# Query tiles 3 and 4 and y tiles 2 and 3 turned by DRAM and VectorE instead of TensorE, with VectorE's turns in PSUM banks

## The chip, the cores and the metric

One core of a Trainium2 chip runs the whole program. The metric is the device time of one execution in microseconds (us); the time of the kernel before is the median of 3 runs.

## What is computed

Two layers, each a linear-attention block followed by a gated MLP that mixes the rows. S = 2048 rows, D = 512 features, 32 heads of 16, Fh = 896, all in fp32.

```python
def A(x, wqkv, wo):                       # linear attention
    q, k, v = split_heads(x @ wqkv)       # 32 heads of 16
    phi = lambda t: where(t > 0, t + 1, exp(t)) + 1e-6
    kv = einsum("hsd,hse->hde", phi(k), v); z = phi(k).sum(rows)
    o = einsum("hqd,hde->hqe", phi(q), kv) / (phi(q) . z + 1e-6)
    return merge_heads(o) @ wo
def B(x, w_in, w_sp, b_sp, w_out):        # gated MLP with spatial mixing
    z = gelu(x @ w_in)
    z1, z2 = z[..., :896], layernorm(z[..., 896:])
    g = w_sp @ z2 + b_sp[:, None]         # over the 2048 rows
    return (z1 * g) @ w_out
for _ in range(2):
    x = x + A(layernorm(x), wqkv, wo)
    x = x + B(layernorm(x), w_in, w_sp, b_sp, w_out)
```

## The kernel before

**Tiling.** The rows are 16 tiles of 128 (NT = 16). An fp32 operand of a matmul is split into a high part (ScalarE, `high`, L220) and a low part (VectorE, `low`, L223), and a product takes three matmuls (`mm3`, L234 to L236: high by high, high by low, low by high). SBUF is handed out in slots: pages (`pg`, 128 x 512), quads (`qd`), bigs (`bg`); PSUM is 8 banks. Each kind has a list of free slots, used in turn. There is no scheduler: every engine runs its instructions in the order in which the code issues them, and a DMA queue (SP's above all) takes its transfers in that order too.

**Stages of a layer.** P1 makes keys, queries and the sums of the attention. P2 (`class P2`) goes over the tiles once more. P4 and its neighbours do the mixing by w_sp in products that are divided further, and the output product.

**P2.** For tile i: the scaled query (`a`, `a2_den`, `a2_mul`, L856 to L877) is turned, so that features lie on the partitions, and split (`b_high`, `b_low`): "q tile i". `c` multiplies it by W2 (12 matmuls), `c2` adds it to x (L911) and takes the statistics (L365, L367 on VectorE, L369 to L372 on POOL), `c3` normalises (ScalarE, L378): "y tile i". That is turned and split as well (`d_high`, `d_low`, into a quad). From it `e` makes the gate half z2 by 24 matmuls of 448 columns, with gelu on ScalarE (L1076) and a normalisation, and `f` makes the other half for four tiles at once. P2's loop runs over steps s; step s issues q tile s, c of tile s-1, y's turn of tile s-2, c3 of tile s-1, `a2` of tile s+2 and e of tile s-3. `run` is layer 0's loop, `run2` layer 1's. From s = 6 on, `run` also issues one or two groups of `f` a step (FONE). POOL and SP in layer 0 also work on sums of parts of w_sp (`sums.tick`: w_sp loads at L202, s stores at L1679) during P2.

**Turning.** `class Turn` knows two ways. A tile named in `by_pe` is turned by four PE transposes (`transposes`, L390) into a PSUM bank, which the split reads; the query's are copied into another order of features first (ScalarE, L421). Any other tile is stored to DRAM on SP (L426), loaded back in another shape on SP (`load`, L202), and turned by one VectorE STREAM_TRANSPOSE (L455) into its `home`: a page for queries, a row-tile slot called z_y for y (`ZHome`), a bank for P1's tiles. Before, q tiles 0 to 4 and y tiles 0, 1, 2, 3 and 15 are in `by_pe`, in both layers. In `run`, where a y tile is in `by_pe` (`late`, L1367), its `d_high` and `d_low` come ahead of `c3`; where it isn't, behind it and behind `a`. `run2` has the same as `ahead`. The load of a turned tile is issued in step s with `qturn.load(s + 2)` and `xturn.load(s - 1)` in layer 0, `qturn.load(s + 1)` at the start of a step in layer 1.

**Mixing's start.** `run` of the mixing class calls for every group of matmuls g: `sp(g + 2)`, which splits a quad of w_sp (ScalarE L1775, VectorE L1778), then `zahead`, which splits pages of z some groups ahead, then `mm(g)` (L2000 to L2002).

Of the kernel before, what the change touches and what calls it, by code (L numbers as in the profile page):

```python
# [19 lines left out]
NT = S // P  # L20
# [98 lines left out]
ACTFROM = 10  # L119
E4LATE = 14  # L120
AHEAD = 14
SPN = 3
LOAD2 = (9, 10, 11, 14)
DVE2 = {12: 1, 13: 1, 14: 2, 15: 2, 16: 2}
# [34 lines left out]
def mixer_kernel(ctx: ExitStack, tc: tile.TileContext, x_in, wqkv, wo_d, win1_d, win2_d, wsp_d, bsp_d, wout_d,  # L159
# [9 lines left out]
    pages = Slots(main, "pg", 22)  # L169
    quads = Slots(main, "qd", 6)  # L170
    bigs = Slots(main, "bg", 4)
    banks = Banks(psum, "bank", 8)
# [231 lines left out]
    class Turn:  # L404

        def __init__(self, name, by_pe, always=False, inbank=False, home=None, copy=True):
            self.name, self.by_pe, self.always, self.inbank, self.home = name, by_pe, always, inbank, home
            self.copy = copy  # L410
            self.held, self.d, self.raw, self.made = {}, {}, {}, {}

# [35 lines left out]
        def pre(self, i):  # L448

            if i in self.made or i not in self.raw:  # L450
                return
            r = self.raw.pop(i)
            home = self.home(i) if self.home else banks if self.inbank else pages
            y = home.get([P, 4, P])
            nc.vector.transpose(y.rearrange("p c (t m) -> p m c t", m=4), r.rearrange("p (m c j) -> p m c j", m=4, c=4))  # L455
            pages.put(r)
            self.made[i] = y, home


    class P1:  # L460
        def __init__(self, L):
            self.L = L
            self.st = 2 * L
            self.x, self.ms, self.xT, self.pk, self.kb, self.r, self.xhl = {}, {}, {}, {}, {}, {}, {}
            self.wk, self.wq = w_square(wqkv, 512), w_square(wqkv, 0, True)
            self.win2 = InSeven() if L else w_in2()
            self.later = deque(range(NT - DEFER, NT))
            self.turn = Turn(f"xt{L}", range(3) if L == 0 else (), False, True)
            self.G = None
            self.zacc = None  # L470
            self.half = None
# [359 lines left out]
    class P2:  # L831
        def __init__(self, p1):
            self.L = L = p1.L
            self.p1 = p1
            self.win1, self.win2 = None if L else w_in1(), p1.win2
            self.ws = deque()
            self.wf = deque([] if not L else [w1parts[f] for f in list(range(NF)) * 2 + [0, 6, 1, 2, 6]]
                            + [w1sums[f, m] for m in range(2) for f in range(3)]
                            + [[t[:, 256:512] for t in w1parts[f + 3]] for f in range(3)])
            self.draw, self.S, self.fdone, self.qhome, self.zacc, self.meant = {}, {}, None, {}, {}, set()  # L840
            self.qturn, self.xturn = Turn(f"qt{L}", range(5), True), Turn(f"yt{L}", (0, 1, 2, 3, NT - 1), home=ZHome, copy=bool(L))
            self.qp, self.qT, self.x, self.ms, self.xB, self.z, self.zms = {}, {}, {}, {}, {}, {}, {}
            self.fq = deque()
            self.fnext = []
            self.A, self.u, self.y = {}, {}, {}
# [484 lines left out]
        def run(self, sums):  # L1330
# [4 lines left out]
            for s in range(1, NT + 3):  # L1335
                if s in (15, 16, 17):
                    self.first_a(s - 15)
                self.loadx(s + 1)
                if s in self.qturn.by_pe:
                    self.c(s - 1)  # L1340
                    self.b_high(s)
                    self.c2(s - 1)
                    self.p1.late_phi_b()
                    self.b_low(s)
                    if s >= 2:
                        self.d_high(s - 2)
                        self.d_low(s - 2)
                    self.p1.late()
                    self.c3(s - 1)
                    self.a2(s + 2)  # L1350
                    self.p1.late_phi_a()
                    self.a(s + 3)
                    sums.tick()
                else:
                    if s < NT:
                        self.b_high(s)
                    self.a2_den(s + 2)
                    if s < NT:
                        self.b_low(s)
                    if s <= NT:  # L1360
                        self.c(s - 1)
                        self.c2(s - 1)
                    if s == NT:
                        quads.put(*self.W2)
                        pages.put(self.zbc)
                    self.a2_mul(s + 2)
                    late = s - 2 in self.xturn.by_pe and s <= NT or AHEAD <= s <= NT  # L1367
                    if s in (NT, NT + 1):
                        self.e(s - 3)
                        self.e2(s - 3)  # L1370
                    if late:
                        self.d_high(s - 2)
                        self.d_low(s - 2)
                    if s <= NT:
                        self.c3(s - 1)
                    self.a(s + 3)
                    if s <= NT + 1 and not late:
                        self.d_high(s - 2)
                        self.d_low(s - 2)
# [99 lines left out]
        def run2(self):  # L1479
            late = self.p1  # L1480
            for s in range(1, NT + 3):
# [2 lines left out]
                self.qturn.load(s + 1)  # L1484
                if s in EXTRA:
                    self.wfetch()
                if s in self.qturn.by_pe:
                    self.c(s - 1)
                    self.b_high(s)
                    self.c2(s - 1)  # L1490
# [217 lines left out]
    class P4:  # L1708
# [622 lines left out]
        def run(self, nxt):  # L2331
            p2 = self.p2
            early = nxt is None
            self.zmade = 0
            n = 0
            for _ in p2.tail():
                n += 1
                if n == 1:
                    self.sums.store()
                self.zahead(n - 1)  # L2340
                self.sp(n - 1)
                if n < 3:
                    self.fetch(n + 3)
            self.zahead(3)
            if not early:
                assert len(self.sums.todo) == LEFT
            self.gb = [bigs.get([P, NF, 512]) for _ in range(NCHK)]
            n = len(self.steps)
            for g in range(n):
                p, k = self.steps[g]  # L2350
                self.fetch(g + 5)
                evac_first = p == "P6" and k == HT - 1
                div_first = p in self.div and k == 13 and p == "P4"
                if not evac_first and not div_first:
                    self.sp(g + 2)
                    self.zahead(g + (3 if p == "P5" else 4))
                self.mm(g)
                if evac_first:
                    self.evac(p)
                    self.sp(g + 2)  # L2360
                if not early and g == TFIRST - 1:
                    self.sums.fetch()
                if not early and TFIRST <= g <= TFIRST + LEFT:
                    self.sums.tick()
                if nxt is not None:
                    self.sums.halve(PARTS.get((p, k), -1), self.mark)
                if p in self.div:
                    if p == "P4" and k == 0 and "P5" in self.div:
                        for j in range(2):
                            nc.gpsimd.tensor_tensor(self.unit(2 + j, 6), self.unit(2 + j, 6), self.unit(j, 6), op=OP.add)  # L2370
                    if k % 2 == 1:
                        self.evac_div(p, self.SEVEN[k // 2])
                    if div_first:
                        self.sp(g + 2)
                    if k == 13 and p == "P4":
                        self.gq.extend((n, f) for n in range(2) for f in range(3))
                    if p == "P5":
                        if k > 10 and k < 13:
                            self.carry(12 - k)
                        if k == 0 or k % 2 == 1:  # L2380
                            self.tick()
                        self.wseven(p, {6: 3, 9: 4, 10: 5, 11: 6, 13: 7}.get(k, -1))
                        if k == 13:
                            self.gq.extend([(n, 3) for n in range(2)] + [(n, 4 + f) for n in range(2) for f in range(3)])
                    continue
                if p == "P1" and k == 6:
                    self.ask(3)
                self.tick()
                if p == "P3":
                    if k == FIRST:  # L2390
                        self.first()
                self.wseven(p, k)
                if p == "P7" and k == HT - 1 and self.div:
                    self.sp(g + 3)
                if k == HT - 1 and not evac_first:
                    self.evac(p, (0,) if p == "P3" else (0, 1))
            pages.put(*self.bs)
            self.out7(nxt)
# [80 lines left out]
```

## Time and profile before

| | |
|---|---|
| median of 3 runs | 1343.82 us (1343.27 to 1344.25) |
| the profiled execution | 1341.83 us |
| its span, first to last instruction | 1340.1 us |
| PE busy | 1334.2 us, 6533 instructions |
| VectorE (DVE) busy | 1074.3 us, 1687 |
| ScalarE (ACT) busy | 739.8 us, 1250 |
| GpSimd (POOL) busy | 464.1 us, 611 |
| moved by DMA | 291.34 MB, 217 GB/s on the mean |
| P2 of layer 0 / of layer 1, the steps spoken of | about 151 to 185 us / 833 to 854 us |

A timeline row is: start, duration (us), engine, line, operation, result and operand by the program's names, partitions by elements, and, in brackets, how long the engine was idle before it and what ended that. "x8" joins eight neighbours. A matmul's duration overlaps with the next one's, so starts tell its cost. "PE bank L619 <- DVE ones_f L185: 1.0, 1, 1.0" in the list of waits reads: PE, about to write a bank at L619, waited for VectorE's result, 1.0 us in all, once, longest 1.0.

### The profile page before, as it was taken

What the parts mean: (1) busy time and instruction counts of PE and PEld (TensorE: products, weight loads), DVE (VectorE), ACT (ScalarE), POOL (GpSimd) and SP (SyncE); (2) the same over time, 40 slices, a digit from 0 to 9 for tenths busy, and PEclk for the clock granted to TensorE, in tenths of its full rate; (3) what the DMA queues carried; (4) which work ended last, traced back from release to release, by engine and by line L of the source; (5) the groups of instructions that cost most, each with busy time, mean ns of one, the idle gap of its engine ahead of it and who ended that gap; (6) DMA issues with size and microseconds to landing.
All of it is one profiled execution on the core that took longest, in us unless ns stands there. A gap on an engine that the chain in (4) does not pass through costs nothing.

```text
span 1340.1 us, 19243 instructions
## 1 busy us (share of the span) xinstructions
PE 1334.2 (100%) x6533; PEld 1138.6 (85%) x6533; DVE 1074.3 (80%) x1687; ACT 739.8 (55%) x1250; POOL 464.1 (35%) x611
## 2 busy tenths in 40 slices
PE   9999999999999999999999999999999999999998
PEld 7888888888888888889988888888888888888898
DVE  7779877767899889898866777777689758899885
ACT  5774544347742265345666655557687333666464
POOL 3765675533036400301422443544441012122021
PEclk9999999999999999999999999999999999999999
DMA  5898489977779986884864552678767455579354
GB/s 184 281 313 275 166 286 313 306 223 250 250 270 378 324 263 216 287 302 79 184 159 138 137 131 88 211 237 269 226 203 246 155 171 174 178 242 322 115 78 65
DMA packets 172594, 291.34 MB, mean 217 GB/s; under 512 B 14544, under 2 KB 53456, under 8 KB 172240
## 3 DMA queue, kind: packets, MB, share of 16 engines
q1 hardware_dynamic: 153376, 250.92, 56.2%
q0 software_dynamic: 18976, 39.07, 13.7%
q8 instruction: 51, 0.84, 0.3%
q14 instruction: 47, 0.39, 0.1%
q10 hardware_dynamic: 144, 0.13, 0.0%
HBM read 205.39 MB, written 101.45 MB: 229 GB/s over the span
## 4 chain that ended last, share of the span: by engine, by line
PE 95%; DMA 2%; DVE 2%; ACT 1%; issue 0%; POOL 0%; SPq 0%; DVEq 0%; ACTq 0%
PE bank L234 13%; PE bank L236 13%; PE bank L235 13%; PE bank L2001 12%; PE bank L2000 12%; PE bank L2002 12%; PE bank L2198 3%; PE bank L2199 3%; PE bank L2200 3%; PE bank L990 1%; PE bank L991 1%; PE bank L992 1%; PE bank L1163 1%; PE bank L1162 1%; PE bank L1161 1%; PE bank L390 1%
## 5 line engine op out<-in xcount | busy, mean ns | idle before, releaser
L2001 PE MATMUL bank<-qd,pg 128*128 128x512 f32 x736 | 286.5, 389 | 0.6 <-DVE qd L1778 0.6
L2002 PE MATMUL bank<-qd,pg 128*128 128x512 f32 x736 | 286.3, 389 | 0.0
L2000 PE MATMUL bank<-qd,pg 128*128 128x512 f32 x736 | 286.3, 389 | 0.0
L1775 ACT ACTIVATE qd<-qd 128x1024 fp32r<-128x1024 f32 x142 | 149.2, 1053 | 125.2 <-PE bank L2002 101.7
L1778 DVE TENSOR_TENSOR qd<-qd,qd 128x1024 fp32r<-128x1024 f32 x132 | 168.6, 1279 | 37.6 <-ACT qd L1775 37.4
L236 PE MATMUL bank<-qd,pg 128*128 128x512 f32 x448 | 174.7, 390 | 0.0
L2001 PEld LDWEIGHTS bank<-qd,pg 128*128 128x128 f32 x736 | 138.1, 188 | 29.5 <-DVE qd L1778 1.0
L2002 PEld LDWEIGHTS bank<-qd,pg 128*128 128x128 f32 x736 | 138.1, 188 | 28.8
L2000 PEld LDWEIGHTS bank<-qd,pg 128*128 128x128 f32 x736 | 138.1, 188 | 28.6
L2041 POOL TENSOR_TENSOR bg<-bg,pg 128x512 f32<-128x512 f32 x28 | 49.8, 1780 | 187.6 <-ACT qd L1775 92.5
L234 PE MATMUL bank<-qd,pg 128*128 128x512 f32 x264 | 103.2, 391 | 0.3 <-ACT pg L220 0.2
L235 PE MATMUL bank<-qd,pg 128*128 128x512 f32 x264 | 102.9, 390 | 0.0
L236 PEld LDWEIGHTS bank<-qd,pg 128*128 128x128 f32 x448 | 84.1, 188 | 18.2 <-DVE pg L223 0.4
L1684 POOL TENSOR_TENSOR pg<-pg,pg 128x512 f32<-128x512 f32 x48 | 70.8, 1476 | 68.7 <-DMA pg<-in_wsp_dram 66.6
L369 POOL TENSOR_SCALAR rs<-mv 128x1 f32<-128x1 f32 x76 | 23.8, 313 | 172.7 <-DVE mv L367 169.0
L2200 PE MATMUL bank<-wo,qd 128*128 128x256 f32 x288 | 81.5, 283 | 0.0
L2198 PE MATMUL bank<-wo,qd 128*128 128x256 f32 x276 | 78.1, 283 | 0.0
L2199 PE MATMUL bank<-wo,qd 128*128 128x256 f32 x276 | 78.0, 283 | 0.0
L220 ACT ACTIVATE pg<-pg 128x512 fp32r<-128x512 f32 (+1 forms) x86 | 50.0, 592 | 45.8 <-DVE pg L1869 19.9
L223 DVE TENSOR_TENSOR pg<-pg,pg 128x512 fp32r<-128x512 f32 (+1 forms) x84 | 54.5, 657 | 11.3 <-ACT pg L220 10.6
L549 POOL TENSOR_TENSOR pg<-pg,pg 128x512 f32<-128x512 f32 x30 | 39.9, 1331 | 55.8 <-DVE pg L543 53.9
L234 PE MATMUL bank<-bg,qd 128*128 128x448 f32 x160 | 59.0, 369 | 0.0
(297 smaller groups left out, 3358.2 us busy)
## 6 DMA issues: line engine op xcount, KB each, us to landing
qd<-s SPq DMA_DIRECT2D x62, 512.0 KB, 4.6
qd<-in_wsp_dram SPq DMA_DIRECT2D x40, 512.0 KB, 4.0
qd<-hP SPq DMA_DIRECT2D x40, 512.0 KB, 4.6
pg<-z SPq DMA_DIRECT2D x56, 256.0 KB, 5.1
pg<-in_wsp_dram SPq DMA_DIRECT2D x52, 256.0 KB, 4.4
s<-pg SPq DMA_DIRECT2D x48, 256.0 KB, 4.0
z<-pg SPq DMA_DIRECT2D x40, 256.0 KB, 3.5
pg<-w POOLq DMA_DIRECT2D x38, 256.0 KB, 4.9
```

The costliest lines, as they stand in the source:

```text
L234: nc.tensor.matmul(out, ah, bh, start=start, stop=False)
L235: nc.tensor.matmul(out, ah, bl, start=False, stop=False)
L236: nc.tensor.matmul(out, al, bh, start=False, stop=stop)
L1684: nc.gpsimd.tensor_tensor(t, a, b, op=OP.add)
L1775: self.mark = nc.scalar.activation(w[:, 0], r, AF.Copy)
L1778: nc.vector.tensor_sub(w[:, 1], r, w[:, 0].bitcast(F32))
L2000: m(out, h[:, o], w[:, 0, j, :], start=start, stop=False, skip_group_check=True)
L2001: m(out, h[:, o], w[:, 1, j, :], start=False, stop=False, skip_group_check=True)
L2002: m(out, l[:, o], w[:, 0, j, :], start=False, stop=stop, skip_group_check=True)
L2198: m(out, A, x, start=start and f == 0, stop=False, skip_group_check=True)
L2199: m(out, A, y, start=False, stop=False, skip_group_check=True)
L2200: m(out, B, x, start=False, stop=stop and f == 2, skip_group_check=True)
```

## The change

Query tiles 3 and 4 and y tiles 2 and 3 leave `by_pe` in both layers: they go by DRAM and VectorE like the later tiles. The branch of a step that the query's `by_pe` selected is now selected by s < 5, so steps 1 to 4 keep their order of work. `Turn` gets `banked`, a set of tiles whose VectorE turn is written into a PSUM bank: q tiles up to 12 in both layers (in place of pages), y tiles up to 12 in layer 0 (in place of z_y); P1's tiles have banks as before. As y tile 3 is no longer in `by_pe`, step 5 issues its `d_high` and `d_low` behind `c3`. In layer 0's mixing the first six groups call `zahead` three groups ahead, not four.

```diff
+QBANK = 13, 13
+YBANK = 13
...
-        def __init__(self, name, by_pe, always=False, inbank=False, home=None, copy=True):
+        def __init__(self, name, by_pe, always=False, home=None, copy=True, banked=()):
...
-            home = self.home(i) if self.home else banks if self.inbank else pages
+            home = banks if i in self.banked else self.home(i) if self.home else pages
...
-            self.turn = Turn(f"xt{L}", range(3) if L == 0 else (), False, True)
+            self.turn = Turn(f"xt{L}", range(3) if L == 0 else (), banked=range(NT))
...
-            self.qturn, self.xturn = Turn(f"qt{L}", range(5), True), Turn(f"yt{L}", (0, 1, 2, 3, NT - 1), home=ZHome, copy=bool(L))
+            self.qturn, self.xturn = Turn(f"qt{L}", range(3), True, banked=range(QBANK[L])), Turn(f"yt{L}", (0, 1, NT - 1), home=ZHome, copy=bool(L), banked=() if L else range(YBANK))
...
-                if s in self.qturn.by_pe:
+                if s < 5:
...
-                    self.zahead(g + (3 if p == "P5" else 4))
+                    self.zahead(g + (3 if p == "P5" or not early and g < 6 else 4))
```

(The line with `if s in self.qturn.by_pe` changes in both `run` and `run2`. Lines of the changed kernel behind the two constants have numbers two higher.)

Where it moves instructions, three places. The first is SP's queue in layer 0's P2, step 3: x_2 is the sum stored by c3(2), qt_5 the fifth query tile on its way through DRAM, yt_2 the y tile, s the parts of w_sp's sums. Before:

```order
L917 DMA x_2_81<-pg_191_1693 128x512
L426 DMA qt_5_1904<-pg_206_1842 128x4x128
L1679 DMA s_145<-pg_198_1760 128x512
L1679 DMA s_2_131<-pg_197_1758 128x512
L202 DMA pg_214_1910<-in_wsp_dram 128x512
L202 DMA pg_215_1912<-in_wsp_dram 128x512
L202 DMA pg_216_1914<-in_wsp_dram 128x512
L202 DMA pg_217_1918<-qt_5_1904 128x512
L202 DMA pg_218_1961<-in_win_dram 128x512
L202 DMA pg_219_1963<-in_x_dram 128x512
```

and in the changed kernel:

```order
L919 DMA x_2_81<-pg_191_1693 128x512
L428 DMA yt_2_1900<-pg_212_1898 128x4x128
L428 DMA qt_5_1907<-pg_205_1844 128x4x128
L1681 DMA s_145<-pg_197_1760 128x512
L1681 DMA s_2_131<-pg_196_1758 128x512
L204 DMA pg_214_1913<-in_wsp_dram 128x512
L204 DMA pg_215_1915<-in_wsp_dram 128x512
L204 DMA pg_216_1917<-in_wsp_dram 128x512
L204 DMA pg_217_1921<-qt_5_1907 128x512
L204 DMA pg_218_1923<-yt_2_1900 128x512
L204 DMA pg_219_1966<-in_win_dram 128x512
```

y 2's store has come in ahead of query 5's store, its load behind query 5's load, where the w_in load stood.

The second place is ScalarE in step 5 of layer 0: the high part of q tile 5 (into z_q), the high part of y 3 (into the quad qd_10), c3(4) (into a page), then work on z. Before:

```order
L220 ACTIVATE bg_5_1766<-pg_208_1852 128x512
L220 ACTIVATE z_q<-pg_228_2072 128x512
L220 ACTIVATE qd_10_1812<-bank_80_2108 128x4x128
L378 ACTIVATE pg_230_2116<-pg_209_1854,nb,rs 128x4x4x32
L378 ACTIVATE z_z_2051<-z_z_2051,nb,rs 128x896
L1076 ACTIVATE z_z_2153<-bank_81_2127 128x448
```

and in the changed kernel:

```order
L222 ACTIVATE bg_5_1768<-pg_208_1856 128x512
L222 ACTIVATE z_q<-bank_79_2075 128x512
L380 ACTIVATE pg_231_2112<-pg_209_1858,nb,rs 128x4x4x32
L222 ACTIVATE qd_10_1814<-bank_81_2118 128x4x128
L380 ACTIVATE z_z_2054<-z_z_2054,nb,rs 128x896
L1078 ACTIVATE z_z_2153<-bank_82_2127 128x448
```

The high part of y 3 has moved behind the normalise of c3(4); on VectorE its turn and its low part are the last of the step, behind the statistics of c2(4).

The third place is ScalarE at the start of layer 0's mixing: the end of the last copies of P2 (L1151), splits of z pages (L220) and of w_sp quads (L1775). Before:

```order
L1151 ACTIVATE pg_376_3947<-bank_148_3810 128x512
L220 ACTIVATE pg_378_3954<-pg_371_3929 128x512
L220 ACTIVATE pg_381_3965<-pg_377_3951 128x512
L1775 ACTIVATE qd_26_3984<-qd_22_3825 128x1024
L220 ACTIVATE pg_383_3987<-pg_380_3962 128x512
```

and in the changed kernel:

```order
L1153 ACTIVATE pg_370_3947<-bank_165_3810 128x512
L222 ACTIVATE pg_372_3954<-pg_365_3929 128x512
L1777 ACTIVATE qd_26_3977<-qd_22_3825 128x1024
L222 ACTIVATE pg_375_3983<-pg_371_3951 128x512
L1939 ACTIVATE bank_168_3999<-bank_166_3962 128x512
```

One split of z that stood ahead of the quad's split stands behind it.

More of the change, by code (lines that the diff above doesn't have):

```diff
@@ L404, in mixer_kernel @@
     class Turn:
-        def __init__(self, name, by_pe, always=False, inbank=False, home=None, copy=True):
-            self.name, self.by_pe, self.always, self.inbank, self.home = name, by_pe, always, inbank, home
+        def __init__(self, name, by_pe, always=False, home=None, copy=True, banked=()):
+            self.name, self.by_pe, self.always, self.banked, self.home = name, by_pe, always, banked, home
             self.copy = copy
@@ L1486, in run2 @@
                     self.wfetch()
-                if s in self.qturn.by_pe:
+                if s < 5:
                     self.c(s - 1)
```

## Prediction

> **What bounds the kernel now.** I read the page first: span, busy times, the granted clock.
>
> ```profile
> span 1340.1 us, 19243 instructions
> PE 1334.2 (100%) x6533; PEld 1138.6 (85%) x6533; DVE 1074.3 (80%) x1687; ACT 739.8 (55%) x1250; POOL 464.1 (35%) x611
> PEclk9999999999999999999999999999999999999999
> ```
>
> TensorE is busy for the whole span at full granted clock, so anything taken from its stream shortens the kernel and anything that makes it wait lengthens it. VectorE is at 80%, so elsewhere there is slack on the average, not in each place. The profiled execution took 1341.83 us, 2.0 under the median of 1343.82; sums are made against the former and 2.0 is added. A difference of 0.2% (2.7 us) is about what a measurement of this kernel tells from none.
>
> Next, the list of PE's waits: four rows, of which this is the longest, at the start.
>
> ```profile
> PE bank L619 <- DVE ones_f L185: 1.0, 1, 1.0
> ```
>
> So no wait inside the stages is there to be removed by faster helpers, but for one in mixing, below. What the change can give is transposes; what it can cost is new waits.
>
> **What the transposes cost TensorE.** The instructions of line L390, then PE's timeline of layer 0 where the affected groups stand: eight transposes (query 4 and y 2) ahead of gate matmuls, four (y 3) ahead of e(2), and e(3).
>
> ```profile
> L390 PE MATMUL bank<-ident,pg x84: 270/272/330, 6.1 to 845.2; 128*128 128x128 f32 x84
> 165.94 1.04 PE L390 MATMUL bank<-ident,pg 128*128 128x128 f32 x8
> 166.73 0.45 PE L234 MATMUL bank<-bg,qd 128*128 128x448 f32 x1
> ...
> 174.41 0.60 PE L390 MATMUL bank<-ident,pg 128*128 128x128 f32 x4
> 174.77 0.45 PE L234 MATMUL bank<-bg,qd 128*128 128x448 f32 x1
> 175.05 0.36 PE L235 MATMUL bank<-bg,qd 128*128 128x448 f32 x1
> 175.25 0.37 PE L236 MATMUL bank<-bg,qd 128*128 128x448 f32 x1
> ...
> 182.57 0.36 PE L234 MATMUL bank<-bg,qd 128*128 128x448 f32 x1
> 182.97 0.36 PE L236 MATMUL bank<-bg,qd 128*128 128x448 f32 x1
> ```
>
> One transpose lasts 272 ns, but they overlap. From the start of a group to the next matmul it is 166.73 - 165.94 = 0.79 for eight and 174.77 - 174.41 = 0.36 for four. The first matmul behind a group holds the next one up by 0.28 (175.05 - 174.77) instead of 0.20 (175.25 - 175.05): 0.08 more. Per layer, query 3 goes from a group of eight shared with y 1 (0.79 to 0.36: 0.43, and I count 0.36), query 4 and y 2 go whole (0.79), y 3 goes whole (0.36); with 0.08 for each of the three: **1.75 a layer, 3.5 in all**. The Trainium skill, "TensorE: Matmul & The Clock Gate", section "Part 4: PE-mode transpose", gives some 275 ns for a transpose inside a kernel, which agrees with the 272 of the row; read as a price that would make 32 transposes 8.7 us. The rows say that this is length, not pitch, so the sum goes by 0.36 and 0.79.
>
> **What lies beside other work: nothing.** Off TensorE, ScalarE drops four reorder copies (L421), and VectorE turns into banks in place of pages. Neither is waited for anywhere in PE's list, so they give nothing by themselves. More banks are held: about seven are taken per step of eight, for about a step each, and are read by one ScalarE and one VectorE instruction; a turn that waits for a bank would show on VectorE. I take 0. The eight added turns are 0.72 each:
>
> ```profile
> L455 DVE STREAM_TRANSPOSE bank<-pg x29: 715/718/727, 26.6 to 781.2; 128x512 f32<-128x512 f32 x29
> ```
>
> **Layer 0, y 2: a load far back in SP's queue.** y 2 now goes to DRAM and back. SP's part of step 3 and the landing times of a neighbour and of all y loads:
>
> ```profile
> 165.25 0.38 SPq L426 DMA_DIRECT2D qt<-pg  x1
> 166.72 1.76 SPq L202 DMA_DIRECT2D pg<-in_wsp_dram  x3
> 169.05 0.38 SPq L202 DMA_DIRECT2D pg<-in_win_dram  x1
> ...
> pg<-in_win_dram SPq DMA_DIRECT2D x1, 256.0 KB, 4.9
> ...
> DMA to landing us min/median/max: 2.3/3.0/6.2
> ```
>
> The store of y 2 enters ahead of query 5's store (165.25), which waits for VectorE in any case, so it is early. Its load comes behind that store, two s stores, three w_sp loads and query 5's load: it takes the place of the w_in load, 169.05. With that load's 4.9 it lands at 173.95; with the shortest landing, 2.3, at 171.4. Then VectorE turns it (0.72), ScalarE takes the high part (0.6), VectorE the low (0.68), some 0.2 for the hand-overs: the low part ends at **176.1** (173.6 to 177.1, the latter if query 3's round trip also shifts VectorE). In the profile it ended at 170.2:
>
> ```profile
> 169.56 0.68 DVE L223 TENSOR_TENSOR qd<-bank,qd 128x512 fp32r<-128x512 f32 x1
> 170.16 0.67 DVE L868 TENSOR_REDUCE den<-pg 128x32 f32<-128x512 f32 x1
> 171.48 0.69 DVE L877 SCALAR_TENSOR_TENSOR pg<-z_q,den 128x512 f32<-128x512 f32 x1
> 173.95 1.15 DVE L365 BATCH_NORM_STATS2 st<-z_z 128x6 f32<-128x448 f32 x2 [1.78 <-ACT z_z L1076]
> 175.31 1.11 DVE L455 STREAM_TRANSPOSE pg<-pg 128x512 f32<-128x512 f32 x1
> 176.27 0.63 DVE L868 TENSOR_REDUCE den<-pg 128x32 f32<-128x512 f32 x1
> 177.43 1.67 DVE L223 TENSOR_TENSOR pg<-pg,z_q 128x512 fp32r<-128x512 f32 x1
> 179.02 0.68 DVE L911 TENSOR_TENSOR pg<-pg,bank 128x512 f32<-128x512 f32 x1
> 180.46 0.18 DVE L367 BATCH_NORM_AGGREGATE mv<-st 128x2 f32<-128x6 f32 x1
> ```
>
> The third matmul of e(2) (L236) needs that low part. It was at 175.25; with 1.75 less ahead of it and no slow follower it is due at 173.4. PE waits **2.7** there (0.2 to 3.7).
>
> **Layer 0, y 3: behind c3(4).** While y 2's turn waits for its data, everything behind it on VectorE waits too, for VectorE works in order; and y 3's turn now stands behind c2(4) and its high part, on ScalarE, behind c3(4). VectorE's work from y 2's low part to the end of c2(4)'s statistics, from the rows above: a2(6) 2.0 (170.16 to 172.17), the z statistics 1.36 (173.95 to 175.31), query 5's turn 0.72 into a bank, the denominator 1.16 (176.27 to 177.43), a low part 0.69 (as long as 1.67 here), c2(4) 1.62 (179.02 to 180.64): 7.6 to 8.5. From 176.1 that is 183.7. Then POOL and ScalarE:
>
> ```profile
> 182.35 0.82 ACT L378 ACTIVATE pg<-pg,nb,rs 128x512 f32<-128x512 f32 x1 [4.77 <-POOL nb L372]
> ```
>
> From the end of the statistics, 180.64, to the end of this normalise, 183.17, it took 2.5; so c3(4) ends at 186.2, and y 3's high and low parts (0.6 + 0.7) end at **187.5**. The third matmul of e(3) was at 182.97 and is due at 181.2. PE's waits in the two places thus add up to **6.3**, the 2.7 among them. Least: if y 2 lands in time, VectorE is still held at the z statistics by ScalarE's gelu of e(1) (its 1.78 of idle), which can come 1.3 earlier (the groups ahead of e(1): 0.44 + 0.87); with 0.4 less for query 5's turn and 1.0 for a low part of 0.69 instead of 1.67, y 3's low part ends at 183.17 + 1.3 - 2.7 = 181.8, 0.6 late. Most, with the upper ends: 8.0. From step 6 on, two first-half groups a step follow e and cover the round trip, as they do now for tiles 4 and above. Layer 0's P2: 6.3 - 1.75 = **+4.55** (-1.15 to +6.25).
>
> **Layer 1, the same two tiles.** Here SP has no w_sp traffic.
>
> ```profile
> 836.37 0.32 SPq L202 DMA_DIRECT2D pg<-qt  x1
> ...
> 838.74 0.68 DVE L223 TENSOR_TENSOR qd<-bank,qd 128x512 fp32r<-128x512 f32 x1
> 845.08 0.69 DVE L223 TENSOR_TENSOR pg<-pg,z_q 128x512 fp32r<-128x512 f32 x1 [0.77 <-ACT z_q L220]
> 847.14 0.18 DVE L367 BATCH_NORM_AGGREGATE mv<-st 128x2 f32<-128x6 f32 x1
> 849.02 0.82 ACT L378 ACTIVATE pg<-pg,nb,rs 128x512 f32<-128x512 f32 x1 [2.89 <-POOL nb L372]
> 853.05 0.36 PE L234 MATMUL bank<-bg,qd 128*128 128x448 f32 x1
> ```
>
> y 2's load goes just ahead of query 5's (836.37), say 835.8, lands at 838.8 with the median of 3.0; turn into z_y (as slow as into a page here, 1.11), high and low end at 841.4, 2.0 later than now and well before e(2). VectorE regains the 0.77 of idle and 0.4 on query 5's faster turn, so the statistics end at 848.2 instead of 847.3, c3(4) 2.5 later at 850.7, y 3's parts at 852.2. e(3)'s third matmul was at 853.05 + 0.4 and is due at 851.7: PE waits some **0.7** (0 to 1.6). Layer 1: 0.7 - 1.75 = **-1.05** (-1.75 to -0.15).
>
> **Mixing's start in layer 0.** ScalarE's and PE's rows:
>
> ```profile
> 352.09 0.63 ACT L220 ACTIVATE pg<-pg 128x512 fp32r<-128x512 f32 x1 [1.31 <-DMA z<-pg]
> 352.63 1.04 ACT L1775 ACTIVATE qd<-qd 128x1024 fp32r<-128x1024 f32 x1
> ...
> 354.04 0.39 PE L2000 MATMUL bank<-qd,pg 128*128 128x512 f32 x1
> 354.99 0.50 PE L2001 MATMUL bank<-qd,pg 128*128 128x512 f32 x1 [0.56 <-DVE qd L1778]
> ```
>
> ScalarE's split of the w quad (L1775) stands behind a z split that waits 1.31 for pages; its low half comes 0.72 late for PE (354.99 against 354.04 + 0.23), and one slow follower adds 0.1. With z one group later this split no longer stands ahead of the quad: **-0.83** (0 if ScalarE then waits for something else).
>
> **Sum:** 4.55 - 1.05 - 0.83 = +2.7 on 1341.83: 1344.5; against the median 1346.5. The bounds of the three terms give 1340.1 to 1349.9.
>
> **Rivals.** *The round trips are hidden* (the other side). If loads land in about 2.3 us and VectorE catches up by c2(4), no wait is left, and the time is 1343.8 - 3.5 - 0.83 = 1339.5. It decides at y 3's low part in layer 0: ready by 181.2 instead of 187.5. For it speaks VectorE's idle time before the z statistics (1.78) and the 4.77 in which ScalarE waits ahead of c3(4); against it the order itself, which puts y 3 behind c3(4), 0.6 late at best. Chance 0.16.
>
> *The clock drops after the gaps.* The start of the kernel shows slow matmuls:
>
> ```profile
> 2.35 3.19 PE L626 MATMUL bank<-pg,ones 128*128 128x512 f32 x8
> ```
>
> Eight took 3.19, where a pitch of 0.23 makes 1.82: 1.4 more. If each of the two gaps in layer 0 were followed by such a stretch, the time would be 1346.5 + 2.8 = 1349.3. Against it: the granted clock shows 9 in all 40 slices, and the wait at 354.99 is short of what would test it. The Trainium skill's "TensorE: Matmul & The Clock Gate", section "What's actually happening", halves the clock after an idle window of about 3.4 us; by that rule gaps of 2.7 and 3.6 us lie at its edge, and no trace here has such a gap inside a stage. Chance 0.07.
>
> *Transposes cost their full length.* Then 32 x 0.272 = 8.7 would go instead of 3.5, and the time would be 1346.5 - 5.2 = 1341.3. The 0.79 for eight refutes it: 0.02. That the change does nothing is excluded: the order has 32 transposes fewer.
>
> **How the numbers follow.** My case has 0.75. Its middle is 1346.5, at the very edge of what counts as slower; the least favourable y 2 landing moves it up by 1 to 2, the median landing of 3.0 instead of 4.9 moves it down by up to 1.9. So of 0.75 I give 0.40 to slower and 0.33 to same, 0.02 to faster. With the hidden case to faster (0.16), the clock to slower (0.07), full length to same (0.02): faster 0.18, same 0.35, slower 0.47. The range: 1339.5 to 1349.9 takes in the hidden case and my upper bounds; my own case alone is 1340.1 to 1349.9.
>
> **What would show it.** In the changed trace, PE should have about 3 us waiting at e(2) of layer 0 and 3 to 4 at e(3), before L236's counterpart, released by VectorE's low part; VectorE's turn of y 2 should idle for its load (some 3 us), and ScalarE's high part of y 3 should follow c3(4) directly. In layer 1 there should be under 1.6 at e(3), and the 0.56 wait in mixing should be gone. PE's transposes should be 60 in number. I am wrong if e(3) in layer 0 runs on without a wait, if a load takes 2.3 where I took 4.9, if turns wait for banks, or if waits appear at tiles 5 and above.

## The result and the profile after

The changed kernel takes 1350.15 us (median of 6 runs, 1348.88 to 1353.76) against 1342.95 (6 runs, 1341.38 to 1344.25): 1.0056 of before, 95% interval 1.0046 to 1.0067. It is slower by 7.2 us where 2.7 was forecast, and just outside the range, which ended at 1349.9. The profiled execution took 1350.8, 9.0 more than the profiled one of before.

The head of the changed kernel's profile, and the list of TensorE's waits:

```profile
span 1349.0 us, 19206 instructions
PE 1335.6 (99%) x6501; PEld 1136.1 (84%) x6501; DVE 1054.9 (78%) x1695; ACT 737.1 (55%) x1246; POOL 458.9 (34%) x611
...
PE bank L236 <- ACT qd L222: 6.7, 3, 3.2
PE bank L238 <- DVE pg L225: 1.1, 2, 0.8
PE bank L621 <- DVE ones_f L187: 1.0, 1, 1.0
PE bank L236 <- DVE pg L225: 0.4, 1, 0.4
PE bank L1163 <- ACT bank L1180: 0.4, 1, 0.4
PE bank L236 <- ACT pg L222: 0.2, 1, 0.2
```

TensorE has 32 instructions fewer; its waits add up to 9.8 us where the four of before made 2.3. The largest new ones, 6.7 us, stand in front of gate matmuls (L236) for the high part of y in a quad. The 0.4 for VectorE at L236 is at 23.20 us, in P1, ahead of everything that the change was priced for. Where the others are, TensorE's timeline of layer 0 shows (start, duration, in brackets the idle time and who ended it; the rows are picked, here and below, and do not follow each other directly):

```profile
154.50 0.39 PE L236 MATMUL bank<-qd,z_h 128*128 128x512 f32 x1
156.91 0.50 PE L238 MATMUL bank<-qd,pg 128*128 128x512 f32 x1 [0.80 <-DVE pg L225]
158.64 0.39 PE L236 MATMUL bank<-qd,pg 128*128 128x512 f32 x1
...
174.87 0.39 PE L238 MATMUL bank<-qd,pg 128*128 128x512 f32 x1
178.11 0.47 PE L236 MATMUL bank<-bg,qd 128*128 128x448 f32 x1 [2.85 <-ACT qd L222]
178.83 0.47 PE L238 MATMUL bank<-bg,qd 128*128 128x448 f32 x1
...
184.39 0.50 PE L238 MATMUL bank<-qd,pg 128*128 128x512 f32 x1 [0.28 <-DVE pg L225]
186.56 0.39 PE L238 MATMUL bank<-qd,pg 128*128 128x512 f32 x1
190.19 0.47 PE L236 MATMUL bank<-bg,qd 128*128 128x448 f32 x1 [3.24 <-ACT qd L222]
190.91 0.74 PE L238 MATMUL bank<-bg,qd 128*128 128x448 f32 x1
191.45 0.57 PE L236 MATMUL bank<-bg,qd 128*128 128x448 f32 x1
194.06 0.37 PE L237 MATMUL bank<-bg,qd 128*128 128x448 f32 x1
```

Read by starts, at the usual pitches of 0.23 and 0.20: four triples from 154.50 to 158.64 take 4.14, where twelve matmuls make 2.75: **1.4** lost in step 2. The third matmul of e(2), 178.83, was due at 174.87 + 0.23 + 0.4 = 175.5: **3.3**. In c(5) 0.55 goes (184.39 was due at 183.72 + 0.23, and the next matmul is 0.1 slow), and e(3)'s third, 190.91, was due at 186.56 + 0.63: 3.7, so **4.25** for e(3). Then seven matmuls from 191.45 to 194.06 take 2.61 instead of 1.42, and the one before them 0.3 more: **1.5** without a wait. There the granted clock, the third number from the end, has fallen:

```profile
180.00:190.00 10.00, 6.67 (x30) 5.13 (x28) 6.98 (x14) 3.04 (x6) 4.93 (x8) 1.00 0.87 284
190.00:200.00 10.00, 9.81 (x38) 8.32 (x39) 6.98 (x14) 3.17 (x7) 6.36 (x10) 0.83 0.83 259
```

The other places are layer 1's e(3), and the end of layer 1's P2:

```profile
859.64 0.39 PE L238 MATMUL bank<-qd,pg 128*128 128x512 f32 x1
860.67 0.47 PE L236 MATMUL bank<-bg,qd 128*128 128x448 f32 x1 [0.64 <-ACT qd L222]
861.40 0.47 PE L238 MATMUL bank<-bg,qd 128*128 128x448 f32 x1
...
983.87 0.39 PE L1165 MATMUL bank<-qd,pg 128*128 128x512 f32 x1
984.66 0.50 PE L1163 MATMUL bank<-qd,pg 128*128 128x512 f32 x1 [0.40 <-ACT bank L1180]
```

That is 861.40 - (859.64 + 0.63) = 1.1 and 984.66 - 984.10 = 0.6. The wait of 0.72 at the start of layer 0's mixing is gone. In all 1.4 + 3.3 + 4.25 + 1.5 + 1.1 + 0.6 - 0.8 - 3.5 = 7.9 of the 8.9 between the two spans. Of the rest 0.4 is lost by 23.20 us in P1, 0.3 around the end of layer 1's P2, and the remainder in small pieces.

Why y comes late, VectorE's, ScalarE's and SP's rows show:

```profile
154.73 0.60 ACT L222 ACTIVATE pg<-bank 128x512 fp32r<-128x512 f32 x1 [3.40 <-DMA qt<-pg]
187.58 0.81 ACT L380 ACTIVATE pg<-pg,nb,rs 128x512 f32<-128x512 f32 x1 [4.32 <-POOL nb L374]
189.53 0.60 ACT L222 ACTIVATE qd<-bank 128x512 fp32r<-128x512 f32 x1 [1.14 <-DVE bank L457]
...
156.17 0.69 DVE L225 TENSOR_TENSOR pg<-bank,pg 128x512 fp32r<-128x512 f32 x1 [2.18 <-DMA s<-pg]
176.70 0.73 DVE L457 STREAM_TRANSPOSE bank<-pg 128x512 f32<-128x512 f32 x1 [5.07 <-DMA pg<-yt]
188.78 0.73 DVE L457 STREAM_TRANSPOSE bank<-pg 128x512 f32<-128x512 f32 x1 [2.33 <-DMA pg<-yt]
...
167.63 0.37 SPq L428 DMA_DIRECT2D qt<-pg  x1
171.39 0.42 SPq L204 DMA_DIRECT2D pg<-yt  x1
178.79 0.38 SPq L428 DMA_DIRECT2D yt<-pg  x1
183.58 0.45 SPq L204 DMA_DIRECT2D pg<-yt  x1
```

y 2's load is issued at 171.39, in the place forecast (forecast 169.05), and VectorE stands 5.07 us until it has landed. That holds up y 2's high part on ScalarE, and c3(3), which follows it; so y 3's store comes only at 178.79, its load at 183.58, and y 3's turn waits for the load 2.33 more.

The rows at 154.73 and 156.17 are another thing. They come from a fourth place where the change moves instructions, which the list ahead of the prediction lacks: SP's queue in steps 1 and 2 of layer 0. The s stores of that time went at once before, and stand behind query 3's store in the changed kernel. SP before:

```profile
146.50 0.88 SPq L1679 DMA_DIRECT2D s<-pg  x2
```

and in the changed kernel:

```profile
151.94 0.38 SPq L428 DMA_DIRECT2D qt<-pg  x1
152.40 0.95 SPq L1681 DMA_DIRECT2D s<-pg  x2
```

ScalarE's high part of q 2 takes the page that q 3's store reads (before, ScalarE's reorder copy had read it), and waits for that store to land; VectorE's low part takes the page of an s store that now stands behind it. This is the 1.4 of step 2. By it VectorE is 1.9 later (156.17 against 154.30 before), and q 3's own turn, at 159.93, adds its 0.73; so a2(5) and query 5's store come 2.4 later (167.63 against 165.25).

### The profile page after: what moved, and what is told of

Its sections match the earlier page's. It is cut to its first block, busy times and chain, and to the rows that moved or that the text cites. A ratio compares the mean times of both kernels' runs of the same rounds, so it can differ in the third digit from the quotient of the medians.

```text
span 1349.0 us, 19206 instructions
## 1 busy us (share of the span) xinstructions
PE 1335.6 (99%) x6501; PEld 1136.1 (84%) x6501; DVE 1054.9 (78%) x1695; ACT 737.1 (55%) x1246; POOL 458.9 (34%) x611
## 5 line engine op out<-in xcount | busy, mean ns | idle before, releaser
L236 PE MATMUL bank<-qd,pg 128*128 128x512 f32 x264 | 103.3, 391 | 0.7 <-DVE pg L225 0.4
L236 PE MATMUL bank<-bg,qd 128*128 128x448 f32 x160 | 59.6, 372 | 6.7 <-ACT qd L222 6.7
```

The costliest lines, as they stand in the source:

```text
L236: nc.tensor.matmul(out, ah, bh, start=start, stop=False)
```

## The experiments

Times are medians of interleaved runs, before beside them on the same chip; "changed" is the kernel with the whole change. Lines of experiments may be shifted by a few.

**y 2 and y 3 back on TensorE.**

```diff
-Turn(f"yt{L}", (0, 1, NT - 1), ...
+Turn(f"yt{L}", (0, 1, 2, 3, NT - 1), ...
```

> The changed kernel with y tiles 2 and 3 back on TensorE; q tiles 3 and 4 still go by DRAM, banks and mixing as changed. Theory (the loss is y's round trip in layer 0's steps 4 to 6, and the clock after it): the gaps of 3.0 and 3.4 us before e(2) and e(3) and the half-clock stretch go, 4 x 0.43 us of transposes stay saved, mixing keeps its 0.83; the wait of about 1.8 us around step 2 (155 to 157 us of the span, TensorE waiting for a low part that waits for a page still being stored) stays. Time 1342.95 - 1.7 + 1.8 - 0.8 = 1342.2. Rival (the q tiles' stores delay everything behind them on SP and are the main cause): gaps of 2 us and more remain at e(2) or e(3), time above 1345.

1342.5 against 1342.99: 0.9996 (0.9987 to 1.0005). One of TensorE's waits:

```profile
PE bank L238 <- DVE pg L225: 0.9, 1, 0.9
```

Both gaps and the slow stretch are gone with y's round trip; the wait of step 2 stays (156.9), query 5's store is as late as in the changed kernel (167.63), and the wait eats most of what q 3 and q 4 save. As the theory said.

**q 3 and q 4 back on TensorE.**

```diff
-Turn(f"qt{L}", range(3), ...
+Turn(f"qt{L}", range(5), ...
```

> The changed kernel with q tiles 3 and 4 back on TensorE; y tiles 2 and 3 still go by DRAM. Theory (y's round trip): the wait around step 2 goes (1.8 us), y 2 and y 3 still come late in layer 0; as a2(5) is no longer delayed by 2.4 us, y 2's load is issued at about 169 instead of 171.4, so the gap at e(2) is about 1 us smaller, the one at e(3) 2 to 3.4, about 5.5 us in the two; 1.7 us of transposes saved, mixing 0.8, layer 1 loses about 1 at e(3). Time 1342.95 - 1.7 - 0.8 + 5.5 + 1 = 1347, and up to 2 more if the clock falls after a gap. Rival (q's stores): the gaps shrink below 1 us and the time is below 1343.

1347.84: 1.0034 (1.0022 to 1.0046). TensorE at e(2), c(5) and e(3):

```profile
176.09 0.47 PE L236 MATMUL bank<-bg,qd 128*128 128x448 f32 x1 [1.42 <-ACT qd L222]
182.37 0.50 PE L238 MATMUL bank<-qd,pg 128*128 128x512 f32 x1 [0.35 <-DVE pg L225]
187.46 0.47 PE L236 MATMUL bank<-bg,qd 128*128 128x448 f32 x1 [2.53 <-ACT qd L222]
```

The wait of step 2 is gone and the gaps are smaller, for query 5's store goes at 165.77 and y 2's load 1.8 us earlier (169.61). The clock falls here too, behind the gap of 2.53: the granted clock of 180 to 190 us is 0.92, that of 190 to 200 us 0.91. So y's route alone makes most of the loss, and the q tiles' route, net of its saved transposes, adds 1350.15 - 1347.84 = 2.3 to it; without y's route it cost nothing, as the run before shows. The 1 us expected at e(3) of layer 1 is not there: its third matmul, at 858.77, is on time. Among the kernels here that matmul is late, by 0.5 to 1.5 us, in the five runs that send all four tiles of layer 1 by DRAM, and on time without the q tiles, as here, or without y 3, as below.

**y's load ahead of the s stores and w_sp loads** (steps 3 and 4 of layer 0; all else as changed).

```diff
                     self.a(s + 3)
+                    self.xturn.load(s - 1)
                     sums.tick()
```

> The changed kernel, with only one thing moved: in steps 3 and 4 of layer 0 y's load is issued ahead of the s stores and w_sp loads on SP, right behind the query's store. Theory (the load's place in SP's queue): y 2's load is issued 3 us earlier, at about 168 instead of 171.4, lands by 172 to 173 instead of 176.6; the gap of 3.0 at e(2) falls below 0.5, c3(3), y 3's store and c2(4) come 3 to 4 us earlier, and what is left at e(3) is the order behind c3(4): 0.5 to 1.5 us, no half-clock stretch. Time 1350.15 - 3.0 - 2.4 - 2.0 = 1342.8. Rival (the round trip itself or VectorE's order is the bound, not the place on SP): both gaps stay above 2 us and the time above 1347.

1347.63: 1.0035 (1.0023 to 1.0047). SP's store and load of y 2, VectorE's turn of it, and TensorE's rows, the granted clock of 180 to 190 us in the last:

```profile
165.09 0.42 SPq L428 DMA_DIRECT2D yt<-pg  x1
170.03 0.33 SPq L204 DMA_DIRECT2D pg<-yt  x1
172.86 0.73 DVE L457 STREAM_TRANSPOSE bank<-pg 128x512 f32<-128x512 f32 x1 [1.31 <-DMA pg<-yt]
...
182.17 0.50 PE L238 MATMUL bank<-qd,pg 128*128 128x512 f32 x1 [1.32 <-DVE pg L225]
183.27 0.63 PE L238 MATMUL bank<-qd,pg 128*128 128x512 f32 x1
185.40 0.63 PE L237 MATMUL bank<-qd,z_q 128*128 128x512 f32 x1
186.70 0.47 PE L236 MATMUL bank<-bg,qd 128*128 128x448 f32 x1 [0.39 <-ACT qd L222]
...
180.00:190.00 10.00, 8.13 (x27) 5.83 (x28) 6.53 (x13) 3.76 (x7) 5.22 (x10) 0.83 0.90 285
```

The chain held, by another route than expected: y 2's turn waits 1.31 instead of 5.07, nothing is left at e(2), 0.39 at e(3). But the load is issued at 170.03, not at 168, for it now waits for y 2's own store, which takes 4.9 to land. It then lands in 2.8 instead of 5.3, so of the 3.9 us that the data come earlier 2.5 are landing time. The time did not follow: only 2.5 us came back, and above 1347 is where the rival had it, though without the rival's gaps. A new wait stands in c(5): a low part on VectorE takes a page that y 3's store still reads. The clock falls behind it (0.43 a matmul from 183.27 to 185.40). Further waits come at the end of P2 and in mixing (1.3 at 322.7, 1.2 at 325.8, 0.9 at 473.3, by starts); that these come from the shifted order of pages is a guess.

**The same without the q tiles**: the last two edits together.

> q tiles 3 and 4 on TensorE, y tiles 2 and 3 by DRAM as changed, and y's load in steps 3 and 4 of layer 0 issued ahead of the s stores and w_sp loads. Theory (y 2's late load holds VectorE up, and all the rest follows): against the same kernel with the load at its changed place (1347.84), the 1.6 at e(2), the 2.7 at e(3) and the slow clock behind it go; 0.5 to 1 of waits stays at e(3) or before it: 1347.84 - 5 = 1343, about as before. Rival (a load further ahead only moves the wait to another holder of pages or of SP): the waits of TensorE in layer 0's steps 5 and 6 stay above 2.5 us in all and the time above 1345.5.

1344.45: 1.0007 (0.9997 to 1.0018). One wait is left in steps 5 and 6:

```profile
183.37 0.47 PE L236 MATMUL bank<-bg,qd 128*128 128x448 f32 x1 [1.11 <-ACT qd L222]
```

From 1347.84 the load's place on SP alone brings back 3.4 us, and the clock stays at 1.00 in this profile. Short of the forecast 1343, but on the theory's side: where the load stands in the queue is the main cause. The place works in two ways of about equal size: the load is issued at 167.15 instead of 169.61, and lands in 2.8 instead of 5.0.

**y 2 alone, y 3 alone** by DRAM, in both layers (by_pe of y (0, 1, 3, 15), or (0, 1, 2, 15); the q tiles on TensorE).

> The changed kernel with only y tile 2 left on the way by DRAM (q 3, q 4 and y 3 back on TensorE), banks and mixing as changed. Theory: y 2's late load leaves 1.6 us at e(2) of layer 0, and VectorE, held up by it, is still late with y 3's low part, 1.5 to 2 at e(3): time 1342.99 - 0.8 - 0.9 + 1.6 + 1.7 = 1344.6. Rival (the loss at e(3) is y 3's own place behind c3(4)): the gap at e(3) is below 0.3, time about 1343.

> The changed kernel with only y tile 3 left on the way by DRAM (q 3, q 4 and y 2 back on TensorE), banks and mixing as changed. Theory (y 3 stands behind c3(4) by the order): nothing at e(2), 1.5 to 2.5 at e(3) of layer 0 even though VectorE is not held up, about 1 in layer 1: time 1342.99 - 0.8 - 0.9 + 2.0 + 1.0 = 1344.3. Rival (e(3) is late only because y 2 holds VectorE up): the gap at e(3) is below 0.5, time about 1342.

y 2 alone: 1345.12, 1.0013 (1.0004 to 1.0022). y 3 alone: 1343.3, 1.0006 (0.9997 to 1.0015). TensorE with y 2 alone, then VectorE's turn and TensorE at e(3) with y 3 alone:

```profile
177.26 0.65 PE L392 MATMUL bank<-ident,pg 128*128 128x128 f32 x4 [2.23 <-ACT pg L380]
```

```profile
181.04 0.73 DVE L457 STREAM_TRANSPOSE bank<-pg 128x512 f32<-128x512 f32 x1 [0.92 <-DMA pg<-yt]
...
182.17 0.39 PE L238 MATMUL bank<-qd,pg 128*128 128x512 f32 x1
183.32 0.47 PE L238 MATMUL bank<-bg,qd 128*128 128x448 f32 x1
```

With y 2 late, y 3's transposes wait 2.23 for c3(3), which stands on ScalarE behind y 2's high part; with y 2 in time, e(3)'s third matmul is 183.32 - (182.17 + 0.63) = 0.5 late, though y 3 stands behind c3(4). The 2 us expected there were a miss, and so was the 1 us in layer 1, where this kernel has no wait: y 3's place costs little alone, and most of its gap in the changed kernel is y 2's lateness passed on. By the medians y 2 and y 3 together cost 4.9, singly 2.3 and 0.5; each of these is uncertain by more than 1 us, and the 4.9 holds the slow stretch of the clock, which the single ones lack (1.00 in both). That the first tile's lateness is passed on to the second is therefore read from the rows, not from the medians.

**The gaps filled** with matmuls whose result is not used, ahead of e(2) and e(3) in layer 0.

```diff
+                    if s in (5, 6):
+                        b = banks.get(PAGE)
+                        for g in range(12):
+                            nc.tensor.matmul(b, self.W2[0][:, g % 4, 0:P], self.W2[0][:, g % 4, :], start=True, stop=True)
+                        banks.put(b)
```

> The changed kernel with 12 extra matmuls of 512 columns (2.7 us of TensorE, their result unused) issued ahead of e(2) and of e(3) in layer 0, where TensorE now stands idle 3.0 and 3.4 us. Theory (the half-clock stretch behind the second gap comes from the idle time): with the gaps filled, the matmuls behind e(3)'s first keep a pitch of 0.20 instead of 0.37, the granted clock of 190 to 200 us is 1.00 instead of 0.83, and the time falls by about 2 us to 1348; the extra matmuls themselves cost at most 0.3. Rival (the slow stretch has another cause, such as the load on memory or power): the stretch stays and the time is 1350 or more. If the filling delays something, the time rises by up to 5.

The slice behind e(3), to be held against the 0.83 above:

```profile
190.00:200.00 10.00, 9.50 (x44) 8.37 (x45) 6.73 (x14) 3.18 (x6) 6.78 (x10) 1.00 0.84 271
```

With TensorE busier the clock stays at 1.00, and the profiled span is 1347.5, 1.5 under that of the changed kernel, although y is as late as there (e(3)'s third matmul at 191.01 against 190.91) and waits of 0.71 and 0.65 are left. It is not one profile alone: the mean granted clock of a whole run is 1.000 in four and 0.999 in two of the six filled runs, and 0.997 to 0.999 in all eleven runs of the changed kernel. So the idle time is what lowers the clock. But the median is 1350.89 (6 runs, 1348.87 to 1354.57; 1.0061, 1.0048 to 1.0075), where 1348 was expected: that the stretch's 1.5 us also show in the median is not shown.

**The changed kernel again.**

> The changed kernel once more, beside the others, since its runs spread over 5 us. Theory (the spread comes from the landing times of the loads and the phase of the clock gate): median 1349 to 1351.5, the gaps at e(2) and e(3) of layer 0 again 2.5 to 4 us each, and in the profile a slow stretch behind one of them or none. Rival (the first profile was a bad one): gaps below 2 us and a median below 1348.

1352.49 (5 runs, 1349.4 to 1352.97), 1.0065 (1.0052 to 1.0078), above the range expected. Its gaps are 3.22 at e(2) and 1.92 at e(3), the latter below the 2.5 expected, and this time the slow stretch follows the first one. The gaps are no accident; how long each is varies by a us or more.

**All four tiles back on TensorE** (banks and mixing as changed), **and only layer 0's tiles back.**

```diff
-Turn(f"qt{L}", range(3), ...
+Turn(f"qt{L}", range(3 if L else 5), ...
-Turn(f"yt{L}", (0, 1, NT - 1), ...
+Turn(f"yt{L}", (0, 1, NT - 1) if L else (0, 1, 2, 3, NT - 1), ...
```

> The changed kernel with q tiles 3, 4 and y tiles 2, 3 all back on TensorE: what is left of the change is the banks for the turns of the later tiles and mixing's z pages one group later. Theory (banks cost nothing, mixing gains its 0.83): time 1342.99 - 0.8 = 1342.2, the 0.72 gap at the start of layer 0's mixing is gone, no new wait in either P2. Rival (the banks take something from TensorE or from the copies at the end of P2, as the new 0.56 at the end of layer 1's P2 hints): waits of TensorE for a bank's reader add up to 1 us or more, time 1343 or more.

> The changed kernel with layer 0's four tiles back on TensorE; layer 1 as changed, banks and mixing as changed. Theory (the loss is all in layer 0, where SP carries the w_sp traffic): no gap above 0.3 at 150 to 200 us, at e(3) of layer 1 0.8 to 1.2, some 0.6 at the end of layer 1's P2; time 1342.99 - 0.8 - 1.75 + 1.1 + 0.6 = 1342.1, the same as before within the measurement. Rival (the route costs as much in layer 1): 1345 or more.

All back: 1342.85 against 1342.78, 1.0000 (0.9991 to 1.0009). Layer 1 only: 1341.24, 0.9988 (0.9980 to 0.9997), the fastest of all kernels tried. A row of the first at the middle of mixing, and one of the second at e(3) of layer 1:

```profile
466.21 0.50 PE L2002 MATMUL bank<-qd,pg 128*128 128x512 f32 x1 [0.71 <-ACT pg L1840]
```

```profile
853.36 0.47 PE L236 MATMUL bank<-bg,qd 128*128 128x448 f32 x1 [0.86 <-ACT qd L222]
```

The banks cost nothing in P2. Mixing's 0.83 is gained at its start and given back, in this kernel, by 1.1 at 461 and 466 us, a wait that neither before nor the changed kernel has. Layer 1 keeps a small gain, 0.12% and barely clear of the noise, although it waits at e(3); the 0.6 expected at the end of its P2 is not there.

**Layer 1 without y 3, then with z in its old place.** The first is the kernel above with y 3 of layer 1 on TensorE as well; the second has `zahead` as before too.

> Layer 0 with all four tiles on TensorE; layer 1 with q 3, q 4 and y 2 by DRAM and y 3 on TensorE; banks and mixing as changed. Theory (in layer 1 q 3, q 4 and y 2 are hidden, y 3 behind a late y 2 alone made the 1.0 at e(3)): no wait above 0.3 in layer 1's P2, 0.87 + 0.44 of transposes saved: 1341.2 or a little less, 0.1% below before. Rival (y 2's turn holds up y 3 here as in layer 0): 1 us or more ahead of y 3's transposes, 1342.5.

> As the kernel before it (layer 0 on TensorE; in layer 1 q 3, q 4 and y 2 by DRAM, banks), but with mixing's z pages in their old place, four groups ahead. Theory (with z one group later, the 0.72 at the start of layer 0's mixing only comes back as 1.1 to 1.7 at 461 to 466 us): the waits at 461 to 466 are gone, the one at about 354 is back, time 1340.5 to 1341.5, the fastest of all. Rival (those waits have another cause): they stay, the early wait comes on top, 1342.5.

1341.73, 0.9994 (0.9985 to 1.0003), and 1341.98, 0.9995 (0.9986 to 1.0004). The wait at e(3) of layer 1 is gone in both. With z in its old place the waits at 461 to 466 are gone, and the early one is back (0.32 at 354.76).

So in the kernels with all four tiles of layer 0 on TensorE the later z trades one wait for the other. It does not do so everywhere: with the q tiles by DRAM (a_yPE) or y 3 alone (k_y3) z is later too, and the waits at 461 to 466 are not there. What decides it is not shown. No kernel is faster than before by the 0.2% that counts, and the last one, expected to be the fastest of all, is not; the lowest median stays that of layer 1 alone, 1.5 us or 0.12%.

## Why the prediction went wrong

**What held.** The gain is the pitch of the transposes, not their length: the group of eight in layer 1 (0.79) is now one of four (0.35), and over its three places that layer regains 1.76 where 1.75 was forecast. A slower kernel was forecast, by gaps at e(2) and e(3) of layer 0 for the reasons given: the load's place on SP, VectorE's turn waiting for it (5.07), and the chain passed on to y 3. Layer 1's wait was sized at 0.7 and is 1.1; the start of mixing gained its 0.83. One detail was otherwise: TensorE stands at the first matmul of e for ScalarE's high part (2.85 and 3.24), not at the third for VectorE's low part, which comes only 0.2 later. The late turn holds both.

**What was sized too small.** "it takes the place of the w_in load, 169.05": the place is right, the time is 171.39, and the landing 5.3 instead of 4.9. That is 2.3 + 0.4 late, of which TensorE's own delay in step 2 hides part: the gaps are 3.3 and 4.25, 7.6 in all, where 6.3 was forecast.

**What was missed.** The step that failed is the one that let q 3 and q 4 go by DRAM at no cost: "What lies beside other work: nothing". Only an upper bound allowed 1 us for query 3's round trip on VectorE. In these rows a page that a store reads was not free until the store had landed, and the next taker was an instruction close behind. ScalarE waited for q 3's page, VectorE for one of the s stores behind it: 1.4 of TensorE in step 2, and 2.4 for query 5's store, which moved y 2's load. With q 3 and q 4 on TensorE that wait is gone and the kernel is 2.3 faster. The prediction looked for such waits at the banks alone, where there are none.

**The clock rival came true in part.** It was given 0.07 as an alternative to the forecast; it came on top of it. It took 1.5 us behind one of the two gaps, not 2.8 behind both. The Trainium skill, "TensorE: Matmul & The Clock Gate", section "What's actually happening", lowers the clock after an idle window of about 3.4 us; the gap of 3.24, with a slow stretch of some 3 us behind it, is close to that, but the clock also fell behind waits of 2.53 and 1.32, which are well under it.

**y 3's place.** The prediction had y 3 late by its place behind c3(4), with "0.6 late at best". Alone, e(3) is 0.5 late, so that bound was near. In the changed kernel it was the load (landed at 183.58 + 5.2 = 188.78) and not the end of c3(4) (188.39) that came last, by 0.4 us.

**Sum.** On the profile, 1.4 of pages, 1.3 more in the two gaps, 1.5 of clock, 0.4 in layer 1, 0.6 at the end of P2 and about 1 in small waits are what the forecast lacks: 2.7 + 6.2 = 8.9.

**What stays open.** What makes the waits at the end of layer 1's P2 and in mixing come and go. Which gaps lower the clock: the length of one does not decide it, for 2.85 did not in the same run in which 3.24 did, and 1.32 did elsewhere. And the changed kernel's spread of 5 us: TensorE's gaps vary, but only two of its runs have a profile. The clock alone does not make the spread, for the filled runs, at 0.999 to 1.000, spread by 5.7 us.

## What to carry to other kernels

A tile that goes through DRAM costs three things besides its transfers: the place of its load in the queue, the page that stays taken until the store lands, and the engines that wait in order for the late turn; find what is queued ahead of the load and who takes the page next. Where two late tiles follow each other, price them together: the first one's lateness is passed on to the second. The same edit can cost much in one layer and nothing in another: in layer 1, whose queue carries no w_sp traffic, it was 1.5 us faster by the medians, too little to count as a gain.

## What the runs showed of the hardware

TensorE's matmuls of 448 columns ran at 0.37 us instead of 0.20 for some 3 us after 3.24 of idle time, and not after 2.85 in the same run. In other runs a slow stretch came after waits of 1.32 (512 columns at 0.43 instead of 0.23), 2.53 and 3.22, and none came after 1.92 (the changed kernel again) or 2.23 (y 2 alone). Filling the idle time kept the granted clock at 1.00. The stores and loads of y 2 and y 3, 256 KB each, took 2.3 to 5.9 us to land in layer 0's P2, so a round trip through DRAM is no constant there.
